# A 32-byte tile ahead of the constants: where three stream buffers begin in SBUF

## The chip, the core and the metric

The kernel runs on one core of one Trainium2 chip; the other cores are idle. The time of a run is in device microseconds (us). Before the change the median of three runs is 812.78 us (812.65 to 812.88). The profiled execution, which all rows below come from, took 812.77 us, of which 811.0 us are its span, from the first to the last instruction; 1.8 us lie around the span.

## What is computed

One token (a vector `x` of 1,024 floats) goes through two branches, and a gate mixes them. Branch A is attention over a long cache: 32 query heads in 4 groups of 8, each group with its own keys and values of 65,536 positions and 128 floats. Branch B is a gated feed-forward network with 3,584 hidden units. Everything is float32.

```
g = sigmoid(sum(x * gate_w))
q = x @ wq                                   # 32 heads of 128
for each of 4 groups (8 heads):
    p = softmax(q_h . k_cache / sqrt(128))   # 65,536 positions
    o_h = p @ v_cache
a = concat(o) @ wo
b = x + (silu(x @ w_gate) * (x @ w_up)) @ w_down * sigmoid(x @ w_r)
out = g * a + (1 - g) * b
```

There is one token, so each weight and each cached key or value is used once or, for a group of heads, by one matmul. 346 MB are read from HBM for an output of 4 KB.

## The kernel before

**One stream.** All large operands are laid end to end into one flow of 128 rows, one for each SBUF partition, in the order of use: for each group the query weights, the keys, the values and the output weights (`PARTS`, line 33), then the three matrices of the feed-forward network. The flow is cut into loads of `LOAD` = 14,336 floats for each partition, which is 57,344 bytes (224 times 256) in each of 128 rows, 7,168 KB in all. The first load, `flow0`, is short (2,048 floats for each partition), and the last two loads are cut into two and six DMAs (`ENDS`, line 51), so that the work on them can begin before the whole load is there. Each of these cuts is a multiple of 256 bytes along the row.

**Three buffers.** The pool `stream` (line 71) holds three tiles of 57,344 bytes for each partition, used in turn. The function `at` (line 88) hands out a slice of the flow. When a slice lies in a load that has not been asked for, `at` takes the next of the three buffers and issues the DMAs of the load on SP's queue (lines 95 and 99). SP executes them in this order. Before each it waits until the buffer's former contents have been read by their last matmul on TensorE.

**What works on the stream.** For each group: `queries` (line 150), `score_chunk` (line 169, 16 matmuls of 128x512 for each of 8 chunks of 8,192 positions, then a copy by ScalarE and a maximum by VectorE), `neg_max`, `value_chunk` (line 197: exponential, transpose, 16 matmuls) and `project` (line 208). Then `up_proj` twice (line 242), and the last matrix at lines 278 to 290, whose last block is worked in two pieces (`PIECES`). After the last matmul VectorE makes `fin` (line 292), and SP sends it out (line 293).

**Where tiles lie.** The pools `const`, `stream`, `scores` and `work` follow one another along each partition, in this order, and each tile takes its size rounded up to 32 bytes. The tiles of `const` lie in the order of their first lines in the code: `xk` from byte 1,152, `x_row` from 1,248, `ident` from 2,272, `ones` from 2,784, then `sel`, `sel8`, `nsel`, `sel4`, `xp`, `qp`, `op`, `hp`, `dots`, `dsum`, `sig`, `rest`, `hid`, and `fin` from 10,464 to 11,488. So the first stream buffer begins at byte 11,488, which is 44 times 256 plus 224. The other two begin 57,344 and 114,688 bytes later, so they too begin 224 bytes after a multiple of 256. All the buffers, and each DMA that goes into one, begin 32 bytes ahead of such a multiple.

Of the kernel before, what the change touches and what calls it, by code (L numbers as in the profile page):

```python
# [8 lines left out]
F32 = mybir.dt.float32  # L9
# [4 lines left out]
P = 128  # L14
# [40 lines left out]
def gated_mix_kernel(ctx: ExitStack, tc: tile.TileContext, x, vecs, flow0, flow, out):  # L55
# [14 lines left out]
    const = ctx.enter_context(tc.tile_pool(name="const", bufs=1))  # L70
# [17 lines left out]
    def at(part, first, n):  # L88

        i, a = divmod(BEGIN[part] + first - FIRST, LOAD)  # L90
        i, a = (i + 1, a) if i >= 0 else (0, BEGIN[part] + first)
        while len(loads) <= i:
            t = stream.tile([P, LOAD], F32, name="st", tag="st")
            if not loads:
                nc.sync.dma_start(t[:, :FIRST], flow0)
            else:
                ends = ENDS.get(len(loads), [LOAD])
                for c0, c1 in zip([0] + ends, ends):
                    nc.sync.dma_start(t[:, c0:c1], flow[len(loads) - 1, :, c0:c1])  # L99
            loads.append(t)  # L100
        return loads[i][:, a : a + n]

    at(("q", 0), 0, 1)

    ident = const.tile([P, P], F32, name="ident")
    make_identity(nc, ident)
    ones = const.tile([P, P], F32, name="ones")
# [221 lines left out]
```

## Time and profile before

| what | before |
|---|---|
| median of 3 runs | 812.78 us (812.65 to 812.88) |
| profiled execution | 812.77 us |
| its span | 811.0 us |
| instructions | 6,755 |
| VectorE busy | 64.3 us |
| ScalarE busy | 45.6 us |
| GpSimd busy | 0.7 us |
| granted TensorE clock, mean | 0.723 |

How to read the rows that follow: engines are PE (TensorE), PEld (its weight loads), DVE (VectorE), ACT (ScalarE), POOL (GpSimd) and SP (SyncE); SPq is SP's queue of DMA issues. A DMA appears in the profile as packets: one for each row of the transfer (here at most 57,344 bytes, into one partition) and one of 4 bytes for each of the 16 DMA engines that marks completion. "Share of 16 engines" is the time that the packets took, over 16 times the length of the window. Packets are counted in the window in which they start, so a short window can show a share a little over 100%. `in_flow` stands for both inputs `flow0` and `flow`, and `st` for the three buffers.

### The profile page before, as it was taken

How to read it: one execution, taken by the hardware profiler on the slowest of the kernel's cores; microseconds unless marked ns; L12 is line 12 of the kernel's file. 1: busy time of each engine (PE TensorE's matmuls, PEld its weight loads, DVE VectorE, ACT ScalarE, POOL GpSimd, SP SyncE). 2: the span in 40 equal slices, each digit the busy share in tenths (PEclk: the TensorE clock that was granted, in tenths of full speed). 3: DMA queues.
4: the chain of work that ended last, by engine and by line, in shares of the span. 5: the costliest groups of instructions: out<-in, count | busy, mean ns of one | idle time of the engine just before them, and what ended most of it. 6: DMA issues, size and time to landing. Idle time of an engine off the chain costs nothing.

```text
span 811.0 us, 6755 instructions
## 1 busy us (share of the span) xinstructions
PE 420.3 (52%) x3142; PEld 127.3 (16%) x3142; DVE 64.3 (8%) x149; ACT 45.6 (6%) x101; POOL 0.7 (0%) x6
## 2 busy tenths in 40 slices
PE   1455454555445564345544545555555544575485
PEld 0111110113101011012110111121111111121132
DVE  2000110000000120000010101000000200000000
ACT  0000020000000020000000300000000200000000
POOL 0000000000000000000000000000000000000000
PEclk9967767678866686666776677767667766677677
DMA  9999999999999999999999999999999999999996
GB/s 415 405 453 419 438 434 424 448 410 448 428 430 439 425 442 422 436 436 422 441 431 436 428 430 436 425 438 442 424 434 428 430 436 427 445 422 436 426 423 276
DMA packets 7963, 346.47 MB, mean 427 GB/s; under 512 B 1016, under 2 KB 1152, under 8 KB 1408
## 3 DMA queue, kind: packets, MB, share of 16 engines
q1 hardware_dynamic: 7784, 346.04, 99.0%
q8 instruction: 24, 0.39, 0.2%
q10 hardware_dynamic: 152, 0.02, 0.0%
q14 instruction: 3, 0.02, 0.0%
HBM read 346.05 MB, written 0.00 MB: 427 GB/s over the span
## 4 chain that ended last, share of the span: by engine, by line
DMA 81%; PE 17%; DVE 1%; issue 0%; SPq 0%; ACT 0%; ACTq 0%
DMA st<-in_flow 81%; PE ps_s L173 7%; PE acc L203 6%; PE ps_f L249 1%; PE ps_q L154 1%; PE att L226 1%; PE ps_m L218 0%; SPq L99 0%; PE ps_m L162 0%; DVE o_sb L214 0%; DVE q_sb L159 0%; ACT s L198 0%; PE ps_m L189 0%; DVE pt L200 0%; DVE mx L179 0%
## 5 line engine op out<-in xcount | busy, mean ns | idle before, releaser
L173 PE MATMUL ps_s<-st,qp 128*32 128x512 f32 x1024 | 154.0, 765 | 150.4 <-DMA st<-in_flow 149.4
L203 PE MATMUL acc<-st,pt 128*32 128x512 f32 x1024 | 155.2, 768 | 140.6 <-DMA st<-in_flow 133.3
L173 PEld LDWEIGHTS ps_s<-st,qp 128*32 128x32 f32 x1024 | 38.2, 136 | 262.1 <-issue 149.1
L203 PEld LDWEIGHTS acc<-st,pt 128*32 128x32 f32 x1024 | 37.3, 136 | 250.7 <-issue 135.4
L178 ACT ACTIVATE s<-ps_s 128x512 f32<-128x512 f32 x32 | 19.1, 597 | 576.7 <-PE ps_s L173 576.7
L249 PE MATMUL ps_f<-st,xp 128*32 128x448 f32 x256 | 34.9, 715 | 26.0 <-DMA st<-in_flow 26.0
L179 DVE TENSOR_REDUCE mx<-s 128x1 f32<-128x512 f32 x32 | 22.0, 686 | 286.4 <-ACT s L178 286.4
L200 DVE STREAM_TRANSPOSE pt<-s 128x512 f32<-128x512 f32 x32 | 22.8, 712 | 191.9 <-PE acc L203 188.2
L154 PE MATMUL ps_q<-st,xp 128*32 128x256 f32 x256 | 23.3, 514 | 18.8 <-DMA st<-in_flow 18.8
L226 PE MATMUL att<-st,op 128*32 128x256 f32 x256 | 20.8, 487 | 13.7 <-DMA st<-in_flow 12.1
L198 ACT ACTIVATE s<-s,nb 128x512 f32<-128x512 f32 x32 | 22.6, 708 | 11.0 <-DVE nb L194 11.0
L280 PE MATMUL y<-st,hp 128*32 128x256 f32 x216 | 16.5, 472 | 5.4 <-DMA st<-in_flow 5.2
L249 PEld LDWEIGHTS ps_f<-st,xp 128*32 128x32 f32 x256 | 9.8, 140 | 50.2 <-issue 27.6
L154 PEld LDWEIGHTS ps_q<-st,xp 128*32 128x32 f32 x256 | 10.0, 144 | 30.7 <-DMA st<-in_flow 20.2
L226 PEld LDWEIGHTS att<-st,op 128*32 128x32 f32 x256 | 9.7, 139 | 23.3 <-DMA st<-in_flow 13.1
L280 PEld LDWEIGHTS y<-st,hp 128*32 128x32 f32 x216 | 7.9, 133 | 13.7 <-DMA st<-in_flow 7.2
L254 ACT ACTIVATE row<-ps_f 128x896 f32<-128x896 f32 x2 | 1.8, 917 | 142.1 <-PE ps_f L249 142.1
L214 DVE COPY o_sb<-acc 128x512 f32<-128x512 f32 x4 | 2.8, 692 | 78.5 <-PE acc L203 78.5
L216 PE MATMUL ps_m<-sel,lb 128*128 128x8 f32 x8 | 1.9, 304 | 10.8 <-DVE lb L212 10.6
L159 DVE COPY q_sb<-ps_q 128x256 f32<-128x256 f32 x4 | 1.7, 425 | 63.6 <-PE ps_q L154 63.6
L189 PE MATMUL ps_m<-md,ones 128*128 128x128 f32 x8 | 2.5, 406 | 8.0 <-DVE md L187 8.0
L218 PE MATMUL ps_m<-sel,o_sb 128*128 128x8 f32 x32 | 5.0, 285 | 2.5 <-DVE o_sb L214 2.5
(55 smaller groups left out, 46.1 us busy)
## 6 DMA issues: line engine op xcount, KB each, us to landing
st<-in_flow SPq DMA_DIRECT2D x45, 7168.0 KB, 42.2
st<-in_flow SPq DMA_DIRECT2D x2, 3072.0 KB, 41.7
st<-in_flow SPq DMA_DIRECT2D x1, 4096.0 KB
st<-in_flow SPq DMA_DIRECT2D x2, 1024.0 KB, 21.9
st<-in_flow SPq DMA_DIRECT2D x1, 2048.0 KB, 36.9
st<-in_flow SPq DMA_DIRECT2D x1, 512.0 KB, 39.7
st<-in_flow SPq DMA_DIRECT2D x1, 384.0 KB, 40.3
st<-in_flow SPq DMA_DIRECT2D x1, 128.0 KB, 34.3
```

What stands on the lines that cost most here:

```text
L154: nc.tensor.matmul(ps[32 * j : 32 * j + 32, :NQ], xp[:, k, :], at(("q", g), k * D + j * NQ, NQ), start=(k == 0), stop=(k == KB - 1),)
L173: nc.tensor.matmul(ps[32 * j : 32 * j + 32, :], qp[:, g % 2, s, :], at(("k", g), c * CH + (4 * s + j) * 512, 512), start=(s == 0), stop=(s ...
L178: nc.scalar.activation(t, ps, AF.Copy)
L179: nc.vector.tensor_reduce(mx[:, c : c + 1], t, AX.X, ALU.max)
L198: nc.scalar.activation(t, t, AF.Exp, bias=nb, scale=SCALE, accum_out=sums[:, c : c + 1])
L200: nc.vector.transpose(pt, t)
L203: nc.tensor.matmul(acc[32 * j : 32 * j + 32, :], pt[:, 32 * m : 32 * m + 32], at(("v", g), c * CH + m * 512, 512), start=(c == 0 and m < 4 ...
L214: nc.vector.tensor_copy(o_sb, acc.rearrange("p (s d) -> p s d", s=4))
L218: nc.tensor.matmul(ps[:, HG : 2 * HG], o_sb[:, s, :], sel[:, HG * s : HG * s + HG], start=(s == 0), stop=(s == 3))
L226: nc.tensor.matmul(att[32 * j : 32 * j + 32, :], op[:, h, :], at(("o", g), h * D + j * NQ, NQ), start=(g == 0 and h == 0), stop=(g == G - ...
L249: nc.tensor.matmul(ps[32 * j : 32 * j + 32, e, :n], xp[:, k, :], at((part, 0), k * F + (2 * j + e) * n, n), start=(k == 0), stop=(k == KB ...
L280: nc.tensor.matmul(y[32 * j : 32 * j + 32, :], hp[:, b, :], at(("down", 0), b * D + j * NQ, NQ), start=(b == 0), stop=False,)
```

## The change

A tile of 128 x 8 floats, `pad`, is taken from `const` after `x_row` and ahead of `ident`. Nothing writes or reads it.

```diff
     at(("q", 0), 0, 1)
 
+
+    const.tile([P, 8], F32, name="pad")
     ident = const.tile([P, P], F32, name="ident")
     make_identity(nc, ident)
     ones = const.tile([P, P], F32, name="ones")
```

Every tile from `ident` on lies 32 bytes further along its partition. The three stream buffers begin at bytes 11,520, 68,864 and 126,208, which are multiples of 256. `fin`, `ident`, `ones`, `sel`, `q_sb` and the eight tiles of scores move from 224 bytes past a multiple of 256 to such a multiple. `xp`, `qp`, `op` and `hp` move from 192 to 224 bytes past one, and the two tiles `pt` from 128 to 160. `xk` and `x_row` stay. The instructions of every engine, their order and their waits are the same in both programs, and so are the arrays in HBM.

## The prediction

> **What bounds the kernel now.** First the page: the busy line of the DMA engines, their queues, and the chain that ended last.
>
> ```profile
> span 811.0 us, 6755 instructions
> PE 420.3 (52%) x3142; PEld 127.3 (16%) x3142; DVE 64.3 (8%) x149; ACT 45.6 (6%) x101; POOL 0.7 (0%) x6
> DMA  9999999999999999999999999999999999999996
> q1 hardware_dynamic: 7784, 346.04, 99.0%
> q8 instruction: 24, 0.39, 0.2%
> DMA 81%; PE 17%; DVE 1%; issue 0%; SPq 0%; ACT 0%; ACTq 0%
> ```
>
> The stream (queue q1) keeps the 16 DMA engines busy for 99.0% of the span, while TensorE works 52% of it. The 17% of the chain on PE could suggest that matmuls hold up the loads, so I look at three loads in a row in TensorE's timeline (start, duration, idle time before).
>
> ```profile
> 671.37 8.48 PE L203 MATMUL acc<-st,pt 128*32 128x512 f32 x56 [8.49 <-DMA st<-in_flow]
> 688.33 8.54 PE L203 MATMUL acc<-st,pt 128*32 128x512 f32 x56 [8.48 <-DMA st<-in_flow]
> 705.28 5.16 PE L203 MATMUL acc<-st,pt 128*32 128x512 f32 x24 [8.41 <-DMA st<-in_flow]
> ```
>
> Loads land every 16.96 and 16.95 us. TensorE works 8.5 us on each and then idles 8.4 to 8.5 us for the next. A landing leads to the release of its buffer 8.5 us later; at that moment one load is half in and one more waits whole in SP's queue, which is why the issue table gives 42.2 us from issue to landing: 8.5 + 16.95 + 16.95 = 42.4. So about 25 us of transfer are always queued ahead of a new issue, and the matmuls on the chain cost nothing. Time is set by how long the rows take on the DMA engines.
>
> ```profile
> st<-in_flow SPq DMA_DIRECT2D x45, 7168.0 KB, 42.2
> st<-in_flow SPq DMA_DIRECT2D x2, 3072.0 KB, 41.7
> st<-in_flow SPq DMA_DIRECT2D x1, 4096.0 KB
> st<-in_flow SPq DMA_DIRECT2D x2, 1024.0 KB, 21.9
> st<-in_flow SPq DMA_DIRECT2D x1, 2048.0 KB, 36.9
> st<-in_flow SPq DMA_DIRECT2D x1, 512.0 KB, 39.7
> st<-in_flow SPq DMA_DIRECT2D x1, 384.0 KB, 40.3
> st<-in_flow SPq DMA_DIRECT2D x1, 128.0 KB, 34.3
> ```
>
> These are 54 DMAs of 128 rows: 6,912 rows, 432 on each of the 16 engines if they share evenly.
>
> **What a row costs beside its bytes.** I take two windows of the DMA view: one in which all rows have 57,344 bytes (40 to 760 us), and one near the end, where they are short (790 to 800 us).
>
> ```profile
> DMA packets 6120, 311.35 MB, mean 432 GB/s; under 512 B 673, under 2 KB 673, under 8 KB 673
> q1 hardware_dynamic: 6096, 310.98, 100.0%
> ...
> DMA packets 292, 4.19 MB, mean 419 GB/s; under 512 B 30, under 2 KB 30, under 8 KB 46
> q1 hardware_dynamic: 292, 4.19, 98.5%
> ```
>
> Long: 6,096 less 673 completion packets are 5,423 rows; 720 us x 16 engines = 11,520 us, or 2,124.3 ns a row. Short: 262 rows of 15,992 bytes on average; 10 us x 16 x 0.985 = 157.6 us, or 601.5 ns a row. The difference is 1,522.7 ns for 41,352 bytes: 0.0368 ns a byte (27.2 bytes per ns and engine). Then 57,344 bytes take 2,111.6 ns, and 12.6 ns are left that each row costs whatever its length, its share of a completion packet included. The rounding of the shares and the edges of the short window make this uncertain by some 3 ns.
>
> **The change part by part.**
>
> *The pad itself* is neither written nor read: no instruction is added or moved and no DMA issued, so no queue is passed and no wait joins. Cost 0.
>
> *The rows written to the stream buffers* are what matters. Before, a row of 57,344 bytes begins 224 bytes after a multiple of 256, so it lies across 225 pieces of 256 bytes, the first filled with 32 bytes and the last with 224. Afterwards it lies in exactly 224. The shorter rows of the last loads begin at the same phase and lose a piece as well. No row of this trace begins at a multiple of 256 in this tile, so the price has to be bounded. From below: 0, if a partly filled piece costs only its filled part; by what comes next, nothing speaks for less than 0 except the rival below. From above: all that a row costs beside its bytes, 12.6 ns x 432 = 5.4 us. In between stands the case that the first piece takes a whole piece's time though 224 bytes of it are empty: 224 x 0.0368 = 8.2 ns a row. It fits inside the 12.6 ns and leaves 4.4 ns for completion packets and the start of a row, which cannot be free; of the two ends the upper one is therefore nearer. I take 8.2 ns: 432 x 8.25 ns = 3.6 us.
>
> [...]
>
> *The other tiles that move* (constants, scores, transposes, the output row) are read and written by engines with time to spare: a load gives TensorE 16.95 us for 8.5 us of matmuls, and DVE and ACT are busy for 8% and 6% of the span. If their accesses became slower, the 8.4 us of idle time hides it; without that cover each added us per load would cost 47 us. Only the end is uncovered:
>
> ```profile
> 807.13 0.64 PE L287 MATMUL y<-st,hp 128*32 128x192 f32 x16 [0.40 <-DMA st<-in_flow]
> 807.84 0.48 DVE L292 SCALAR_TENSOR_TENSOR fin<-y,rest,x_row 128x256 f32<-128x256 f32 x1 [22.85 <-PE y L287]
> 808.35 0.65 SPq L293 DMA_DIRECT2D out<-fin  x1
> ```
>
> Of these 3.9 us from the last landing to the end of the span, the shift touches 0.64 + 0.48 us of engine work: even 10% either way is 0.1 us. I take 0.
>
> *Where the gain goes.* All 16 engines save the same on each row, and with 25 us queued ahead none runs dry. Buffers come free 0.07 us earlier per load (8 rows x 8.2 ns), landing, matmuls and next issue moving together, so nothing is late in place of it.
>
> **Sum.** Against the profiled execution: 812.77 - 3.6 = 809.2 us (span 811.0 - 3.6 = 807.4, with the same 1.8 us around it). The profiled time is 0.01 us from the median of 812.78, so the forecast for the median is 809.2 us.
>
> **The rivals.**
>
> *Only what is read counts (no change).* The row's 12.6 ns may be made of work at its start and of the completion packets alone. For it: the data cannot separate a fixed cost from an unaligned piece, since every stream row has both. Against it: a large part of a time as long as that of 342 bytes (12.6 / 0.0368) would need another reason. Time: 812.8, within 0.3 of it. That the change does not do what it says is no separate case: with the constants summed up, the buffers do begin at 11,520 and so on.
>
> *Another limit takes over half-way.* If reading a row from HBM has a start cost of its own, overlapped today with the empty part of the first written piece, the gain ends when the two are equal. The 4.4 ns that I leave over is the nearest number: the gain shrinks to 8.2 - 4.4 = 3.8 ns a row, 1.7 us, 811.1. For it: reading and writing of one row must overlap, or 27 bytes per ns would not be kept up; against it: nothing shows two limits so close together.
>
> *Slower: SBUF writes collide with matmul reads.* DMA pieces would begin at the same phase as the strips of 2,048 bytes that TensorE reads from the neighbour buffer, and writes would wait in the time that PE is busy.
>
> ```profile
> 40.00:200.00 160.00, 82.64 (x620) 23.77 (x620) 13.08 (x25) 9.93 (x23) 0.00 (x0) 0.71 1.00 433
> 200.00:400.00 200.00, 98.72 (x732) 28.77 (x728) 15.96 (x37) 11.12 (x25) 0.00 (x0) 0.71 1.00 431
> 400.00:600.00 200.00, 107.98 (x748) 31.18 (x740) 16.63 (x34) 12.31 (x27) 0.00 (x0) 0.71 1.00 433
> 600.00:760.00 160.00, 86.50 (x602) 25.16 (x606) 12.20 (x26) 9.25 (x22) 0.00 (x0) 0.69 1.00 433
> ```
>
> The last column (GB/s) varies by 2 of 432, 0.5%, between these stages; if such a loss came over the whole stream it would cost 4 us: 816.8. It decides from 1.63 us on, 0.39% of TensorE's 420.3 busy us. Against it: the rate does not fall with PE's share (52%, 49%, 54%, 54%; the lowest rate stands beside the lowest share), and strips and rows had one common phase before, too.
>
> **How the numbers follow.** The full price: 0.42. Half-way: 0.14, and as 1.7 us lies on the bound of 0.2% (1.63 us; that is about what a measurement of this kernel tells from no change), a little over half of it counts as faster. No change: 0.30. Slower: 0.14. So faster 0.50, same 0.36, slower 0.14. The likeliest time is 809.2. From below the range is bounded by all 12.6 ns gone (807.3, which I give 3% and cut at 808.0); upward it takes in no change with its 0.3 us: 813.2. It leaves out most of the slower case. The likeliest case's own range is 808.0 to 810.8 (4.5 to 11 ns a row).
>
> **What would show each step right or wrong.** In the changed profile the landings of full loads should be 16.88 to 16.89 us apart instead of 16.95, the 40-to-760 window should hold about 5,445 rows at 2,116 ns each, and the mean rate there rise by 0.4%, to 434 GB/s. If TensorE's idle time before a load grows instead, or landings are further apart in all stages alike, the stream has become slower, and my price has the wrong sign. If landings stay at 16.95 us, a row's fixed cost has nothing to do with where it begins in SBUF, and the first rival holds. About 16.92 us speaks for the half-way case. A shorter time with the same landings would mean that the gain came from the last 4 us or from the first load, where I have put nothing.

## The result, and the profile after

The changed kernel takes 810.37 us (median of 7 runs, 810.19 to 810.46) against 812.78 us before (812.65 to 812.88): 2.41 us less, a ratio of 0.997 with a 95% interval of 0.9959 to 0.9982. The profiled execution took 810.41 us, with a span of 808.6 us.

The page of the changed kernel, the same parts as before:

```profile
span 808.6 us, 6755 instructions
PE 413.6 (51%) x3142; PEld 125.3 (16%) x3142; DVE 64.3 (8%) x149; ACT 45.6 (6%) x101; POOL 0.7 (0%) x6
q1 hardware_dynamic: 7784, 346.04, 99.0%
q8 instruction: 24, 0.39, 0.2%
DMA 82%; PE 16%; DVE 1%; issue 0%; SPq 0%; ACT 0%; ACTq 0%
```

Packets, bytes and the share of the DMA engines are the same, in a span 2.4 us shorter: the same rows took less time. TensorE's timeline shows it at three loads in a row (start, duration, idle time before):

```profile
669.60 7.82 PE L205 MATMUL acc<-st,pt 128*32 128x512 f32 x56 [9.19 <-DMA st<-in_flow]
686.47 7.91 PE L205 MATMUL acc<-st,pt 128*32 128x512 f32 x56 [9.06 <-DMA st<-in_flow]
703.38 4.56 PE L205 MATMUL acc<-st,pt 128*32 128x512 f32 x24 [8.99 <-DMA st<-in_flow]
```

The landings are 16.87 and 16.91 us apart instead of 16.96 and 16.95. Three landings are few for a difference of some hundredths, so the same timeline is read over a long stretch, from the landing of load 1 to that of load 44. First the kernel before, then the changed one:

```profile
22.73 5.10 PE L154 MATMUL ps_q<-st,xp 128*32 128x256 f32 x48 [13.77 <-DMA st<-in_flow]
...
756.21 8.73 PE L249 MATMUL ps_f<-st,xp 128*32 128x448 f32 x64 [5.55 <-DMA st<-in_flow]
```

```profile
22.55 5.34 PE L156 MATMUL ps_q<-st,xp 128*32 128x256 f32 x48 [13.63 <-DMA st<-in_flow]
...
754.15 8.21 PE L251 MATMUL ps_f<-st,xp 128*32 128x448 f32 x64 [6.05 <-DMA st<-in_flow]
```

43 loads took 733.48 us before and 731.60 us after: 1.88 us less for 344 rows on each DMA engine, 5.5 ns a row. The whole 2.41 us over 432 rows are 5.6 ns a row. The end is as it was, from the last landing to the output's DMA:

```profile
804.77 0.64 PE L289 MATMUL y<-st,hp 128*32 128x192 f32 x16 [0.34 <-DMA st<-in_flow]
805.48 0.48 DVE L294 SCALAR_TENSOR_TENSOR fin<-y,rest,x_row 128x256 f32<-128x256 f32 x1 [23.13 <-PE y L289]
805.99 0.65 SPq L295 DMA_DIRECT2D out<-fin  x1
```

0.64, 0.48 and 0.65 us, each as before, though `fin` and `hp` lie elsewhere. All of the gain came from the stream: outside the long stretch 0.53 us are left for the other 88 rows on each engine, 6.0 ns a row.

The two windows of the DMA view that gave a row's cost beside its bytes, in the changed kernel (40 to 760 us, and 788 to 798 us, where the rows are as short as they were from 790 to 800):

```profile
DMA packets 6131, 312.00 MB, mean 433 GB/s; under 512 B 672, under 2 KB 672, under 8 KB 672
q1 hardware_dynamic: 6106, 311.61, 100.0%
...
DMA packets 290, 4.20 MB, mean 420 GB/s; under 512 B 29, under 2 KB 29, under 8 KB 41
q1 hardware_dynamic: 290, 4.20, 98.1%
```

5,434 rows in 11,520 us are 2,120.0 ns each; 261 rows of 16,092 bytes in 157.0 us are 601.4 ns. The slope is again 0.0368 ns a byte, and 9.0 ns are left beside the bytes, where 12.6 were before, each uncertain by some 3 ns. The price of a byte has not moved, only that of a row.

The packed traces also hold the duration of every single packet, which the views above do not list. Of the 5,760 rows of 57,344 bytes, 95.5% take 2,116 ns in the changed kernel. In the kernel before 7.6% take that long, 66% take 2 to 5 ns more and 26% take 8 to 12 ns more. The mean over all these rows falls from 2,123.4 to 2,118.4 ns, and the durations of all the stream's rows add up to 799.8 us on each engine, where they were 802.1. So the rows themselves last less long, and the 5 to 6 ns are a mean: single rows paid different amounts.

### The profile page after: what moved, and what is told of

Same layout as the page of the kernel before. It is cut to its first block, busy times and chain, and to the rows that moved or that the text cites. A ratio compares the mean times of both kernels' runs of the same rounds, so it can differ in the third digit from the quotient of the medians.

```text
span 808.6 us, 6755 instructions
## 1 busy us (share of the span) xinstructions
PE 413.6 (51%) x3142; PEld 125.3 (16%) x3142; DVE 64.3 (8%) x149; ACT 45.6 (6%) x101; POOL 0.7 (0%) x6
## 4 chain that ended last, share of the span: by engine, by line
DMA 82%; PE 16%; DVE 1%; issue 0%; SPq 0%; ACT 0%; ACTq 0%
DMA st<-in_flow 82%; PE ps_s L175 7%; PE acc L205 6%; PE ps_q L156 1%; PE att L228 1%; PE ps_f L251 1%; PE ps_m L220 0%; SPq L99 0%; DVE o_sb L216 0%; PE ps_m L164 0%; DVE q_sb L161 0%; ACT s L200 0%; DVE pt L202 0%; DVE mx L181 0%; PE y L289 0%
## 5 line engine op out<-in xcount | busy, mean ns | idle before, releaser
L205 PE MATMUL acc<-st,pt 128*32 128x512 f32 x1024 | 150.9, 750 | 145.6 <-DMA st<-in_flow 138.3
L251 PE MATMUL ps_f<-st,xp 128*32 128x448 f32 x256 | 32.6, 675 | 28.2 <-DMA st<-in_flow 28.2
L200 ACT ACTIVATION_READ_ACCUMULATOR s<-s,nb 128x1 f32 x32 | 6.0, 186 | 0.0
```

The lines of the kernel that those rows point to most:

```text
L200: nc.scalar.activation(t, t, AF.Exp, bias=nb, scale=SCALE, accum_out=sums[:, c : c + 1])
L205: nc.tensor.matmul(acc[32 * j : 32 * j + 32, :], pt[:, 32 * m : 32 * m + 32], at(("v", g), c * CH + m * 512, 512), start=(c == 0 and m < 4 ...
L251: nc.tensor.matmul(ps[32 * j : 32 * j + 32, e, :n], xp[:, k, :], at((part, 0), k * F + (2 * j + e) * n, n), start=(k == 0), stop=(k == KB ...
```

## The experiments

Times are compared within one set of runs on one chip, where the kernel before was run as well: 812.99, 812.78, 813.02 and 812.96 us in the four sets. Three kernels with aligned buffers stand 2.4 to 2.5 us under it. In sets without such a kernel "aligned" below means the time before less 2.41 us, the difference of the result.

### Which tile, and which phase

The first kernel moves the stream alone: the 32 bytes stand behind the last constant.

```diff
     fin = const.tile([P, NQ], F32, name="fin")
+    const.tile([P, 8], F32, name="pad")
```

> The 32 bytes come behind the last constant, so the constants stay where they were and only the stream's buffers, the scores and the work tiles move; the buffers begin at multiples of 256. If the gain of 2.4 us belongs to the rows that the DMAs write into the stream's buffers: 810.4 us, rows of 57,344 bytes at 2,120 ns as in the changed kernel. If it belongs to the constants (stationary operands, the identity, the output row): 812.8 us and 2,124 ns.

Measured: 810.51 us (810.44 to 810.82), ratio 0.997 (0.9959 to 0.9981). The constants had not moved, and the gain is there. It belongs to what the DMAs write into the stream's buffers.

Three more kernels have the pad of the change in other sizes, so that the buffers begin elsewhere:

```diff
+    const.tile([P, 16], F32, name="pad")   # 32 after a multiple of 256; [P, 40]: 128; [P, 56]: 192
     ident = const.tile([P, P], F32, name="ident")
```

> The pad has 64 bytes, so the buffers begin 32 bytes after a multiple of 256. Theory A (the empty part of the first 256-byte piece costs its time, 0.0368 ns a byte, and a floor of 2.6 ns a row from another limit hides the first part of it; the floor is 8.2 ns less the 5.6 ns that 2.4 us make on 432 rows): 1.2 ns are empty, under the floor, so 810.4 us as at 0. Theory B (any unaligned row pays for one piece more, the same price at every phase): 812.8 us. Theory C (only a start at an odd multiple of 32 bytes costs, multiples of 64 are free): 812.8 us.

> The pad has 160 bytes, so the buffers begin 128 bytes after a multiple of 256. Theory A (empty part of the first piece, with a floor of 2.6 ns): 4.7 - 2.6 = 2.1 ns a row, 0.9 us, so 811.3 us. Theory B (one piece more, same price at every phase but 0): 812.8 us. Theory C (multiples of 64 are free): 810.4 us.

> The pad has 224 bytes, so the buffers begin 192 bytes after a multiple of 256. Theory A (empty part of the first piece, with a floor of 2.6 ns): 7.1 - 2.6 = 4.4 ns a row, 1.9 us, so 812.3 us. Theory B (one piece more, same price at every phase but 0): 812.8 us. Theory C (multiples of 64 are free): 810.4 us.

| buffers begin after a multiple of 256 by | median, us | above aligned (810.51), us | per row, ns |
|---|---|---|---|
| 32 bytes | 812.97 (812.84 to 813.09) | 2.46 | 5.7 |
| 128 bytes | 812.42 (812.33 to 812.76) | 1.91 | 4.4 |
| 192 bytes | 812.58 (812.49 to 812.71) | 2.07 | 4.8 |
| 224 bytes (before) | 812.99 (812.89 to 813.12) | 2.48 | 5.7 |

Theory A, which keeps the prediction's reason and adds a floor, falls with the first line: at 32 bytes hardly anything of the first piece is empty, and the row costs as much as at 224. Without the floor the prediction's own price would be 1.2 ns a row there, 0.5 us, and falls as well. Theory C falls with the lines for 128 and 192. Theory B, one more piece at about one price, is left, though 128 and 192 are 0.4 to 0.6 us cheaper than it says. The landings of the kernel with 32 bytes are those of the kernel before, in TensorE's timeline:

```profile
671.51 8.56 PE L204 MATMUL acc<-st,pt 128*32 128x512 f32 x56 [8.48 <-DMA st<-in_flow]
688.47 8.62 PE L204 MATMUL acc<-st,pt 128*32 128x512 f32 x56 [8.40 <-DMA st<-in_flow]
705.44 5.23 PE L204 MATMUL acc<-st,pt 128*32 128x512 f32 x24 [8.36 <-DMA st<-in_flow]
```

16.96 and 16.97 us. Its single rows are spread like those of the kernel before, too: 6.6% take 2,116 ns, 67% take 2 to 5 ns more and 26% take 8 to 12 ns more.

### Which side: HBM or SBUF

Both kernels lay the rows of the flow in HBM 224 bytes further, in rows of 57,600 bytes; one has the buffers of the kernel before, the other those of the changed kernel.

```diff
-                nc.sync.dma_start(t[:, :FIRST], flow0)
+                nc.sync.dma_start(t[:, :FIRST], flow0[:, 56 : 56 + FIRST])
...
-                    nc.sync.dma_start(t[:, c0:c1], flow[len(loads) - 1, :, c0:c1])
+                    nc.sync.dma_start(t[:, c0:c1], flow[len(loads) - 1, :, 56 + c0 : 56 + c1])
```

> The changed kernel (buffers at multiples of 256), but each row of the flow in HBM is laid 224 bytes after a multiple of 256, in rows of 57,600 bytes of which 57,344 are read. Runs so far: any start off a multiple of 256 in SBUF costs about 2.4 us. If only the SBUF side counts: as the changed kernel, about 2.4 us under the kernel before, 810.5 us. If what counts is whether both ends have the same phase: 813 us. [...]

> The kernel before (buffers 224 bytes after a multiple of 256) with the rows in HBM at the same phase of 224. If only the SBUF side counts: as the kernel before, 813 us. If what counts is whether both ends have the same phase: 810.5 us. If both sides count and add up: 816 us or more; if both count and the slower one sets the pace: 814 us.

Measured: 810.39 us (810.21 to 810.5) with aligned buffers, 812.75 us (812.69 to 812.89) with those of the kernel before, which itself took 812.78 us in this set. Moving the rows by 224 bytes in HBM changes nothing, alone or together with the phase in SBUF. So the 2.4 us belong to the written side. The address at which an array begins in HBM is not visible here. Of two phases that differ by 224 at most one can be a multiple of 256. If neither is, a cost that is the same at both would not show; so it is not shown that every start in HBM is free. The prediction's price for the empty part of a first piece does not describe what was measured on either side. On the written side a start at 32 costs as much as one at 224 (2.46 and 2.48 us). On the HBM side, with pieces at multiples of 256 there as well, the move would have added 224 empty bytes to each row if the rows began at a multiple of 256 before, and taken away 32 if they began 32 bytes or more past one. At 0.0368 ns a byte that is an estimate of 3.6 us more or 0.5 us less, and the times moved by 0.03 us at most. The 816 and 814 us expected where both sides count are the same 3.6 us on top of the kernel before and the changed one; neither was seen.

### A price of each row

Each full load is cut into four DMAs, so that there are 3.5 times as many rows for the same bytes; once with the buffers of the kernel before, once with the pad.

```diff
-                ends = ENDS.get(len(loads), [LOAD])
+                ends = ENDS.get(len(loads), [LOAD // 4, LOAD // 2, 3 * LOAD // 4, LOAD])
```

> The kernel before with each of the 45 full loads cut into four DMAs of 14,336 bytes a row: 1,080 rows more on each DMA engine (1,512 instead of 432), the same bytes. If the start of a row costs, at every row: 8.4 ns that the changed kernel's rows cost beside their bytes less 3.8 ns of instruction fetches are 4.6 ns, with 5.6 ns on top for the unaligned start and 0.8 ns of a completion packet about 11 ns x 1,080 = 11.9 us more, 824.7 us, and 8.4 us above the same cut with aligned buffers (1,512 x 5.6 ns). If the cost of the unaligned start belongs to a load or to its bytes and not to a row: 2.4 us above the same cut with aligned buffers.

> The changed kernel with each of the 45 full loads cut into four DMAs of 14,336 bytes a row. 1,080 more rows on each engine at 4.6 ns and 0.8 ns of a completion packet: 5.8 us more than the changed kernel, 816.3 us. If a row's cost beside its bytes came from the unaligned start alone, nothing more: 810.5 us.

Measured: 824.12 us (824.0 to 824.35) at 224, 816.23 us (816.11 to 816.26) aligned, 7.89 us apart. The gap has grown 3.3 times (from 2.4 us) with 3.5 times as many rows (1,512 against 432): 5.2 ns a row. The price is one of the row, not of the load or of its bytes. The aligned pair tells what stays: 816.23 us less the 810.39 us of the aligned kernel of the same set are 5.84 us for 1,080 rows, 5.4 ns a row with its share of a completion packet. In the traces before and after, a completion packet of the stream lasts 9.0 ns, 1.1 ns for each of the 8 rows that a DMA has on one engine, where the expectation took 0.8. Its 3.8 ns of instruction fetches agree with q8's 0.2% of 16 engines' span before, spread over 6,912 rows. Queue line of the page, first at 224, then aligned:

```profile
span 822.6 us, 6891 instructions
...
q1 hardware_dynamic: 27224, 346.05, 99.5%
```

```profile
span 814.4 us, 6891 instructions
...
q1 hardware_dynamic: 27224, 346.05, 99.4%
```

Equal packets and bytes, nearly equal shares, and 8.2 us between the spans: in both, the packets fill the engines' time; at 224 they last longer. The trace has 541.1 ns for the mean row of 14,336 bytes at 224 and 535.6 ns aligned.

### The start, or the number of pieces

With buffers at multiples of 256, the rows of the 45 full loads (360 of the 432) are made longer by padding that nothing reads: at the end, at the beginning, at both, or by a whole piece at the end. The buffers and the rows in HBM have 256 bytes more for it (in HBM 512 where both ends grow). In the cut below, `base` and `front` stand for the number of floats by which the load's own data begin later in the buffer and in HBM; the kernels have numbers there. The kernel with both ends is made from the kernel before, with `base` 8 in place of the pad, so that its data begin at the same byte 11,520.

```diff
-                    nc.sync.dma_start(t[:, c0:c1], flow[len(loads) - 1, :, c0:c1])
+                    l, h = (0, 8) if len(ends) == 1 else (0, 0)   # start: (8, 0); both: (8, 8); whole piece: (0, 64)
+                    nc.sync.dma_start(
+                        t[:, base + c0 - l : base + c1 + h], flow[len(loads) - 1, :, front + c0 - l : front + c1 + h]
+                    )
```

> The changed kernel, with the rows of the 45 full loads 32 bytes longer at their end (57,376 bytes; the 32 bytes are padding that nothing reads): they begin at a multiple of 256 and end 32 bytes after one, across 225 pieces. The bytes alone cost 32 x 0.0368 x 360 rows = 0.4 us. If the unaligned start is what costs: 810.9 us. If it is the number of pieces (225 for 224), or an end off a multiple: 360 x 5.5 ns = 2.0 us on top, 812.8 us.

> The changed kernel, with the rows of the 45 full loads 32 bytes longer at their beginning (57,376 bytes): they begin 32 bytes ahead of a multiple of 256 and end at one, across 225 pieces as well, with the same bytes as the kernel with the longer end. If the unaligned start is what costs: 812.8 us, 2.0 us above that kernel. If the number of pieces costs: 812.8 us for both. If only an end off a multiple costs: 810.9 us.

> The rows of the 45 full loads are 32 bytes longer at either end (57,408 bytes, padding that nothing reads): they begin 32 bytes ahead of a multiple of 256 and end 32 bytes after one, across 226 pieces, two of them with 32 bytes only. The bytes alone cost 64 x 0.0368 x 360 rows = 0.85 us above the changed kernel, so 811.4 us. If each incomplete piece costs its own 5.6 ns: 2 x 2.0 us on top, 815.4 us. If a row pays once, whenever it is not made of whole pieces: 2.0 us on top, 813.4 us.

> The changed kernel with rows of 57,600 bytes in the 45 full loads, 256 bytes longer at the end: 225 whole pieces, beginning and ending at multiples of 256. If only the bytes cost: 256 x 0.0368 x 360 = 3.4 us above the changed kernel, 814.0 us; that is 9.4 ns for a 225th piece that is full, against 6.8 ns (1.2 for the bytes and 5.6) for one with 32 bytes. If rows of this length cost 5.6 ns for another reason, such as the padded rows in HBM: 816.0 us.

| rows of the full loads | pieces | median, us | above aligned, us | per row (of 360), ns |
|---|---|---|---|---|
| 32 bytes more at the end | 224 whole, one of 32 | 813.04 (812.91 to 813.22) | 2.4 | 6.8 |
| 32 bytes more at the start | one of 32, 224 whole | 812.98 (812.86 to 813.1) | 2.4 | 6.6 |
| 32 bytes more at both | 224 whole, two of 32 | 815.43 (815.32 to 815.48) | 4.9 | 13.6 |
| 256 bytes more at the end | 225 whole | 813.91 (813.81 to 814.09) | 3.4 | 9.3 |

A row that begins at a multiple of 256 but ends off it pays as much as one that begins off it: the start is nothing special. In the kernel with the longer end the matmuls read at the same phases as in the changed one, so the cost does not come from their reads. Two small pieces cost twice one. A whole piece costs its bytes (256 x 0.0368 = 9.4 ns) and no more. The landings of the last two kernels in TensorE's timeline agree, both ends first:

```profile
674.11 7.85 PE L206 MATMUL acc<-st,pt 128*32 128x512 f32 x56 [9.19 <-DMA st<-in_flow]
691.13 7.88 PE L206 MATMUL acc<-st,pt 128*32 128x512 f32 x56 [9.16 <-DMA st<-in_flow]
708.14 4.47 PE L206 MATMUL acc<-st,pt 128*32 128x512 f32 x24 [9.14 <-DMA st<-in_flow]
```

```profile
672.52 8.15 PE L208 MATMUL acc<-st,pt 128*32 128x512 f32 x56 [8.82 <-DMA st<-in_flow]
689.47 8.21 PE L208 MATMUL acc<-st,pt 128*32 128x512 f32 x56 [8.80 <-DMA st<-in_flow]
706.43 4.83 PE L208 MATMUL acc<-st,pt 128*32 128x512 f32 x24 [8.75 <-DMA st<-in_flow]
```

17.02 and 17.01 us for rows of 57,408 bytes, 16.95 and 16.96 us for rows of 57,600: the longer row is the faster one.

**One estimate fits the mean row of all the runs:** a row takes as long as if it were written in pieces that end at multiples of 256 bytes in SBUF, each at 0.0368 ns a byte (the slope of the two windows), but not less than about 6.8 ns (the measured price of one of 32 bytes, from the rows with a longer end). An unaligned row of 57,344 bytes replaces one whole piece (9.4 ns) by two parts. Parts of 32 and 224 bytes: 6.8 + 8.2 - 9.4 = 5.6 ns, measured 5.7. Two of 128: 6.8 + 6.8 - 9.4 = 4.2, measured 4.4. Parts of 64 and 192: 6.8 + 7.1 - 9.4 = 4.5, measured 4.8. The price of a piece of 32 bytes is put into this fit, so only the four phases test it. That the smallest time is the same for pieces between 32 and 128 bytes is an assumption; the runs with 128 and 192 agree with it to 0.3 ns, 0.13 us in the total. It is a fit of means alone: at one and the same phase single rows pay from nothing to 12 ns, which a fixed smallest time does not explain. What in the chip sets these times is not shown.

## Why the prediction was right, point by point

- **The bound.** Right: DMA engines at 99.0% in both, 25 us of transfer always queued ahead, and matmuls on the chain that cost nothing. That loads landed faster and the whole 2.4 us arrived at the end confirms it; nothing else came late in its place.
- **Where the change acts.** Right: on the rows written to the stream's buffers alone. Moving the stream without the constants gave the whole gain, and the tail's three steps last as long as before.
- **The price of a row.** This is the step that was off. The term of the sum was 224 x 0.0368 = 8.2 ns, for a first piece that takes a whole piece's time though 224 of its bytes are empty. It measured 5.6 ns, and its reason fell too: at 32 bytes past a multiple almost nothing would be empty, and the price is the same. The row crosses 225 pieces for 224, as the prediction counted, but an incomplete piece costs less than a whole one (6.8 ns for 32 bytes, 9.3 for a whole piece), and the empty bytes do not set its price. The sign named for this step fell short as well: 5,434 rows at 2,120.0 ns in the long window, not 5,445 at 2,116. The forecast of 809.2 us was 1.2 us too low for this. That 810.37 us still lies within the likeliest case's own range of 4.5 to 11 ns a row is owed to the width of that range, not to the reason given for the price.
- **The bound from above.** 12.6 ns of a row's cost beside its bytes were taken from two windows, with some 3 ns of uncertainty. The runs give 5.6 ns for the alignment and 5.4 ns for a row and its completion. The prediction overlooked a third part, which is not the row's own: the packets of queues q8 and q14, which the page lists as "instruction" (24 and 3 packets, 0.39 and 0.02 MB). In the trace before, 26 of the 5,760 full rows lasted 0.1 to 0.7 us longer than the median, 25 of them while a packet of these two queues was on its way; spread over all rows that is 2.2 ns. Together this is 13.2 ns, the 12.6 within their uncertainty. Beside the alignment there were thus 7.6 ns, not the 4.4 that the prediction left over, so the argument by which it chose the upper end was about 3 ns short.
- **The rivals.** No change and a slower stream were not seen. The half-way case came nearest in size (1.7 us foretold, 2.4 measured), but not by its reason: a floor under which the empty part hides would have made the start at 32 bytes free, and it cost 2.46 us. That reading and writing of one row overlap, the argument for this case, was an inference from the rate; no run shows it.
- **Only what is read counts**, the name of the first rival, would have meant no gain. The side that is read showed no cost at the two phases tried (0.03 us at most for a move of 224 bytes), and the written side has one (2.41 us for a move of 32).

## What to carry to other kernels

Where a kernel is bound by its loads, look at where in SBUF each row of a DMA begins and ends: an incomplete 256-byte piece at either end costs up to 5.6 ns more than its bytes here, on the mean row, and none of the four offsets tried was free. A pad of 32 bytes in front of the buffers removed it here (812.78 to 810.37 us); lengthening the rows to whole pieces instead would not have paid (9.3 ns measured for a whole last piece, 6.8 for one of 32 bytes). The number of rows sets how much it is: 2.4 us of 812.8 with 432 rows on each engine, 7.9 us with 1,512. Moving the start of the rows in HBM by 224 bytes made no difference here.

## What the runs showed that was not expected

Rows of 57,600 bytes passed faster than rows of 57,408 (813.91 us against 815.43 us). The place of a row in HBM did not matter (810.39 us with the rows moved by 224 bytes). And an aligned row still costs 5.4 ns beside its bytes, completion included, so that cutting loads into four costs 5.8 us even where nothing is misaligned.
